# Raw weight pairs of the gated layer: two alternating pairs of buffers in place of one, and an earlier place for their loads

## The chip, the cores and the metric

The kernel runs on one core of a Trainium2 chip. The metric is the device time of one execution in microseconds (us). The kernel before takes 925.53 us (median of three runs, 925.38 to 925.86).

## What is computed

Three stages follow one another: retention (attention with a decay in place of the softmax), a feed-forward layer with the Mish function, and a gated feed-forward layer (SwiGLU). All is float32.

```python
scores = q @ k.T / sqrt(64)                       # 4 batches, 8 heads, 576 positions
ret = scores * Dmat                               # causal, gamma[h] ** (i - j)
x = (ret @ v), heads joined                       # [2304, 512]
h = x @ w_in                                      # [512, 2048]
x = (h * tanh(softplus(h))) @ w_out               # [2048, 512]
g = x @ w_gate;  val = x @ w_val                  # [512, 1536] each
out = (silu(g) * val) @ w_out2                    # [1536, 512]
```

## The kernel before

**Numbers in two parts.** TensorE multiplies a rounded float32 format. So every factor is split into a high and a low part, and a product is three matmuls. ScalarE makes the high part (a cast), VectorE the low one (a subtraction).

**Four stretches of time.** First comes retention. Then come the slots `slot(s)` of the first layer, up to s = 63: each does one first-layer product (12 matmuls, L610) and one older second product (12 matmuls, L644), some 4.2 us together. Then come the *joint blocks* `pair1(i)`, i = 0 to 7 (L914). They compute the last two token blocks of the first layer together, by a Strassen scheme of seven products in place of eight. Product c of pair i is six matmuls at L839 into a PSUM tile `te`; after it a few waiting matmuls of the second product (L881, mostly 9 or 12) are taken from a list. The last stretch is the gated layer, also by Strassen (L1057, tiles `t`).

**What hangs on a product of a joint block.** Three PSUM tiles rotate through two buffers. Each product c is followed by one operation that empties or reads its tile: a ScalarE copy (c = 0), a Mish on ScalarE (c = 2) or an addition on VectorE (L846, c = 1, 3, 4, 5, 6). The product two places later (c + 2) can't begin before that operation is done.

**Weights of the gated layer.** Each Strassen product needs a combination of weight blocks, in two parts. These are made ahead of time on ScalarE and VectorE, in pieces strewn between the first layer's work, and stored to device memory (`comb`); the gated layer reads them back. `group(n)`, n = 0 to 11, prepares one pair of raw weight tiles, gate (even n) or value (odd n). Its `load` issues two 512 KB loads (L186) into the buffers `raw0` and `raw1`. Its steps are: two `rebias` steps (L114 on ScalarE, L115 on VectorE, on the raw words), two times `sign` and `join` (L119, L123), and then puts and combinations in turn. A put (L189) casts into one of four `c` tiles on ScalarE (L191), subtracts on VectorE (L192), and has SyncE write the tile to `comb` (L193). A group puts seven: a11 and a12, a22, s1 and s3, s2 and s4.

**Who else has raw buffers.** There are four, `raw0` to `raw3`. `last(n)`, n = 0 to 3, prepares one weight tile of the last product in `raw2`. `group1(i)`, i = 0 to 7, makes combinations of the first layer's weights and uses `raw3` as scratch (`e`).

**Order and pace.** The order on every queue is written out by hand: what the program emits first runs first on its engine. `pieces()` (L276) strings the groups together. Each step has a price; `Pace` (L292) gets a credit per slot or per product (2.0 per slot, 1.2 per slot from s = 51 on and per product of pairs 1 to 7) and emits steps while the credit lasts. A step of price 0.0 (the loads) is emitted as soon as it is reached. A group's twelve steps cost 8.6; the load of the next group follows them, and then `gap`, two empty steps of 0.8, before the next group's first `rebias`. By these prices group 6 ends in slot 60, group 7 runs from slot 62 to product (1,5), that is pair 1, c = 5, and groups 8 to 11 fill products (2,0) to (6,4). `group1(7)` ends in slot 58.

**The SyncE queue** issues all of these transfers in one order: the raw loads, the writes to `comb`, and the loads of the first layer's stored combinations (`eu`, L720, 512 KB, one after every second product, six tiles ahead). An instruction that waits there holds up all behind it.

Of the kernel before, what the change touches and what calls it, by code (L numbers as in the profile page):

```python
# [16 lines left out]
def retention_mish_swiglu(  # L17
# [48 lines left out]
    def cols(w, i):  # L66
        return w.bitcast(U32)[:, i * 256:(i + 1) * 256].rearrange("(k p) f -> p k f", p=128)
# [18 lines left out]
    def place(kind, i, shape, dtype, name):  # L86
        j = home[kind, i]
        return pools["a" if j < NA else "b"].tile(shape, dtype, tag=f"u{j}", name=name)

    def words(j):  # L90
        w = raw[j].rearrange("p (n t) -> p n t", t=2)
        return w[:, :, 0], w[:, :, 1]
# [19 lines left out]
    def rebias_raw(j):  # L112
        lo, hi = words(j)
        nc.scalar.activation(hi.bitcast(F32), hi.bitcast(F32), AF.Copy, scale=2.0 ** -112)  # L114
        nc.vector.tensor_scalar(lo, lo, 29, None, op0=ALU.logical_shift_right)  # L115

    def sign(j):
        lo, hi = words(j)
        nc.vector.scalar_tensor_tensor(lo, hi, 0x80000000, lo, op0=ALU.bitwise_and, op1=ALU.bitwise_or)  # L119

    def join(j):
        lo, hi = words(j)
        nc.vector.scalar_tensor_tensor(lo, hi, 3, lo, op0=ALU.logical_shift_left, op1=ALU.bitwise_or)  # L123
# [60 lines left out]
    def raw_load(key, src, whole, n):  # L184
        raw[key] = rp.tile([128, 2 * DM], U32, tag=f"raw{n}", name=f"raw{key}")
        nc.sync.dma_start(out=raw[key] if whole else raw[key].rearrange("p (k f) -> p k f", k=KT), in_=src)  # L186


    def put(x, dst, nm, eng):  # L189
        c = pools["c"].tile([128, 2, KH], F32R, tag="c", name=nm)  # L190
        nc.scalar.copy(out=c[:, 0, :], in_=x)  # L191
        eng.tensor_tensor(out=c[:, 1, :], in0=x, in1=c[:, 0, :].bitcast(F32), op=ALU.subtract)  # L192
        nc.sync.dma_start(out=dst, in_=c.bitcast(F32))  # L193
# [5 lines left out]
    def combine(v, names):  # L199
        for o, a, b, op in ADDS:  # L200
            if o in names:
                nc.vector.tensor_tensor(out=v[o], in0=v[a], in1=v[b], op=op)

    def group(n):
        i, z = divmod(n, 2)
        keys = [f"{'gv'[z]}{i}_{e}" for e in range(2)]
        v = {}

        def load():
            for e in range(2):  # L210
                raw_load(keys[e], cols((w2_gate, w2_val)[z], 2 * i + e), False, e)
                lo, hi = words(keys[e])
                for h in range(2):
                    v[f"a{e + 1}{h + 1}"] = lo[:, h * KH:(h + 1) * KH].bitcast(F32)
                    v["s" + "1324"[2 * e + h]] = hi[:, h * KH:(h + 1) * KH].bitcast(F32)

        def puts(*names):
            for nm in names:
                c = z * NG + USES.index(nm)
                put(v[nm], comb[i][c // 2][:, c % 2], f"c{i}_{c}", nc.vector)  # L220

        return load, [
            (0.55, lambda: rebias_raw(keys[0])), (0.55, lambda: rebias_raw(keys[1])),
            (0.7, lambda: sign(keys[0])), (0.7, lambda: join(keys[0])),
            (0.7, lambda: sign(keys[1])), (0.7, lambda: join(keys[1])),
            (0.85, lambda: puts("a11", "a12")), (0.85, lambda: combine(v, ("s1", "s3"))),
            (0.45, lambda: puts("a22")), (0.85, lambda: combine(v, ("s2", "s4"))),
            (0.85, lambda: puts("s1", "s3")), (0.85, lambda: puts("s2", "s4")),
        ]
# [29 lines left out]
            (0.85, lambda: combine(v, ("s2", "s4"))), (0.85, lambda: puts("s2", "s4")),  # L259
        ]  # L260

    FIRST = 4

    def last(i):
        key = f"f{i}"

        def puts():
            x = words(key)[0].bitcast(F32)
            for h in range(DM // KH):
                put(x[:, h * KH:(h + 1) * KH], find[i][:, :, h * KH:(h + 1) * KH], f"f{i}_{h}", nc.gpsimd)  # L270

        return lambda: raw_load(key, rows(w2_out, i), True, 2), [
            (0.6, lambda: rebias_raw(key)), (0.7, lambda: sign(key)), (0.7, lambda: join(key)), (0.2, puts),
        ]

    def pieces():  # L276
        gr = [group(n) for n in range(2 * PAIRS)]
        gap = [(0.8, lambda: None)] * 2
        for n, (load, steps_) in enumerate(gr):
            f_load, behind = last(n) if n < FIRST else (None, gap)  # L280
            if n == 0:
                yield 0.0, load
                yield from gap
            yield from steps_[:2]
            if f_load:
                yield 0.0, f_load
            yield from steps_[2:]
            if n + 1 < len(gr):
                yield 0.0, gr[n + 1][0]
            yield from behind  # L290

    class Pace:  # L292
# [3 lines left out]
        def __call__(self, more):  # L296
            self.left += more
            while self.ahead and self.left >= self.ahead[0]:
                self.left -= self.ahead[0]
                self.ahead[1]()  # L300
                self.ahead = next(self.todo, None)

    second = Pace(pieces())
    third = Pace(x for i in range(F1 // 2) for x in group1(i))

# [297 lines left out]
    with tc.manual_schedule():  # L603
# [128 lines left out]
        def fin_load(i):  # L732
            at_ = ("in", 1 + i) if i < 8 else ("out", 4 + i)
            fu[i] = place(*at_, [128, 2, DM], F32R, f"fu{i}")
            if i < FIRST:
                nc.sync.dma_start(out=fu[i].bitcast(F32), in_=find[i])

        def fin_raw(i):
            if i < F2:
                key, shape = f"f{i}", [128, 2 * DM]  # L740
                raw[key] = place("in", 9, shape, U32, f"raw{key}") if i % 2 else pools["rx"].tile(
                    shape, U32, tag="rx", name=f"raw{key}"
                )
                nc.sync.dma_start(out=raw[key], in_=rows(w2_out, i))

        def fin_step(u, c):
            n = FIRST + 2 * (u - 1)
            i, k = divmod(c, 4) if c < 4 else (1, c - 3)
            i += n
            key = f"f{i}"  # L750
            if k == 0:
                rebias_raw(key)
            elif k == 1:
                sign(key)
            elif k == 2:
                join(key)
                fin_load(i)
                nc.scalar.copy(out=fu[i][:, 0, :], in_=words(key)[0].bitcast(F32))
            else:
                nc.vector.tensor_tensor(  # L760
                    out=fu[i][:, 1, :], in0=words(key)[0].bitcast(F32), in1=fu[i][:, 0, :].bitcast(F32), op=ALU.subtract
                )
                fin_raw(i + 2)
            if c == 3:
                rebias_raw(f"f{n + 1}")
# [236 lines left out]
        later += rests  # L1002
        for i in range(FIRST):
            fin_load(i)
        fin_raw(FIRST)
        fin_raw(FIRST + 1)
        nc.scalar.preload_act_table_set("silu_and_others")
# [109 lines left out]
        for u in range(NS2):  # L1117
            i = u % PAIRS
            if i == PAIRS - 2 and u + 2 < NS2:
                n = u // PAIRS + 1  # L1120
# [65 lines left out]
```

## Time and profile before

| | us |
|---|---|
| median of three runs | 925.53 |
| the profiled execution | 924.93 |
| its span, first to last instruction | 923.1 |
| TensorE busy | 906.4 (98%) |
| VectorE busy | 564.0 (61%) |
| ScalarE busy | 379.5 (41%) |
| span of the joint blocks, first `te` product to first `t` product | 357.2 to 490.3 |

The profile is of one execution. The page gives each engine's busy time; a weight load (PEld) runs beside the matmuls (PE), so both are near full where TensorE is never idle. The timeline lists instructions in order of time; in square brackets stands how long the engine was idle before one, and what released it. The windows give the engines' busy time in chosen stretches. An operation's duration includes its latency, and operations in a row overlap by some 0.1 us.

### The profile page before, as it was taken

The numbers are of one execution on the slowest core, as the hardware profiler recorded it, in microseconds if no ns is written. First come the engines' busy times: TensorE is split into PE (matmuls) and PEld (weight loads), VectorE is DVE, ScalarE is ACT, GpSimd is POOL, SyncE is SP. The second block draws the span as 40 slices with busy tenths as digits, with TensorE's granted clock in tenths as the row PEclk, the third lists the DMA queues.
The fourth block names the chain that finished last, engine by engine and source line by source line (L and its number), as shares of the span: only waits on it lengthen the run. The fifth ranks groups of instructions, "written<-read, shape, count | busy, mean of one in ns | idle before, by whom it ended". The sixth has DMA issues, their size and how long they took to land.

```text
span 923.1 us, 15226 instructions
## 1 busy us (share of the span) xinstructions
PE 906.4 (98%) x5828; PEld 862.3 (93%) x5828; DVE 564.0 (61%) x1094; ACT 379.5 (41%) x790; POOL 58.3 (6%) x55
## 2 busy tenths in 40 slices
PE   8999999999999999998999999999999999999998
PEld 8888999999999999988999999999999999999997
DVE  3878599468867773555684666656544556544444
ACT  3767466355555544434454333324222223222222
POOL 3654200000000000000000000000000000000000
PEclk9999999999999999999999999999999999999999
DMA  9999265267876636577657566544644444654421
GB/s 213 252 256 235 70 185 181 80 205 264 281 253 229 234 140 219 194 252 264 227 194 296 175 211 202 187 155 159 218 160 158 163 156 164 219 160 160 160 92 68
DMA packets 125016, 177.58 MB, mean 192 GB/s; under 512 B 46352, under 2 KB 83984, under 8 KB 124944
## 3 DMA queue, kind: packets, MB, share of 16 engines
q1 hardware_dynamic: 123840, 176.19, 61.0%
q8 instruction: 46, 0.75, 0.3%
q10 hardware_dynamic: 1104, 0.42, 0.2%
q14 instruction: 26, 0.21, 0.1%
HBM read 133.07 MB, written 43.52 MB: 191 GB/s over the span
## 4 chain that ended last, share of the span: by engine, by line
PE 82%; DMA 6%; DVE 6%; ACT 3%; issue 1%; SPq 1%; DVEq 0%; ACTq 0%
PE t L839 28%; PE fa L1019 16%; PE h L610 14%; PE acc L644 13%; PE te L839 3%; PE ea L881 3%; PE o L513 2%; DMA rawg<-in_moe_w_gate_dram 1%; DMA rawv<-in_moe_w_val_dram 1%; DMA q<-in_q_dram 1%; DMA raw<-in_moe_w_out_dram 1%; PE acc L852 1%; PE s L437 1%; DMA comb<-c 1%; PE o L504 1%
## 5 line engine op out<-in xcount | busy, mean ns | idle before, releaser
L839 PE MATMUL t<-y,su 128*128 128x384 f32 x1512 | 306.7, 338 | 1.1 <-ACT p L1091 0.6
L839 PEld LDWEIGHTS t<-y,su 128*128 128x128 f32 x1512 | 270.8, 188 | 24.4 <-DVE cv L846 1.8
L1019 PE MATMUL fa<-fu,g 128*128 128x512 f32 x648 | 190.2, 395 | 0.1
L610 PE MATMUL h<-xs,u 128*128 128x384 f32 x768 | 143.7, 336 | 0.0
L644 PE MATMUL acc<-g,u 128*128 128x384 f32 x720 | 134.6, 336 | 0.4 <-DVE u L134 0.4
L610 PEld LDWEIGHTS h<-xs,u 128*128 128x128 f32 x768 | 133.9, 188 | 0.4
L644 PEld LDWEIGHTS acc<-g,u 128*128 128x128 f32 x720 | 125.8, 188 | 0.7 <-DVE u L134 0.7
L1019 PEld LDWEIGHTS fa<-fu,g 128*128 128x128 f32 x648 | 118.5, 188 | 7.7 <-ACT g L1042 0.5
L1042 ACT CAST g<-sg 128x384 fp32r<-128x384 f32 x72 | 37.0, 513 | 173.2 <-DVE sg L1078 120.5
L881 PE MATMUL ea<-ge,u 128*128 128x256 f32 x576 | 77.3, 281 | 0.0
L881 PEld LDWEIGHTS ea<-ge,u 128*128 128x128 f32 x576 | 75.4, 189 | 0.0
L839 PE MATMUL te<-ye,eu 128*128 128x384 f32 x336 | 68.4, 338 | 6.0 <-DVE ve L846 2.8
L672 DVE TENSOR_TENSOR g<-m,g 128x384 fp32r<-128x384 f32 x64 | 36.0, 563 | 60.1 <-ACT g L668 60.0
L1067 ACT ACTIVATE sg<-sg 128x384 f32<-128x384 f32 x54 | 28.4, 526 | 90.9 <-DVE sg L846 90.9
L1047 DVE TENSOR_TENSOR g<-sg,g 128x384 fp32r<-128x384 f32 x72 | 40.2, 558 | 40.7 <-ACT g L1042 40.7
L839 PEld LDWEIGHTS te<-ye,eu 128*128 128x128 f32 x336 | 56.9, 188 | 7.0 <-DVE ve L846 3.2
L661 ACT ACTIVATE m<-h 128x384 f32<-128x384 f32 x64 | 31.2, 488 | 66.7 <-PE h L610 66.7
L846 DVE TENSOR_TENSOR u<-t,p 128x384 f32<-128x384 f32 x36 | 20.0, 556 | 44.2 <-PE t L839 41.4
L846 DVE TENSOR_TENSOR v<-t,p 128x384 f32<-128x384 f32 x36 | 20.0, 556 | 35.4 <-PE t L839 34.7
L668 ACT CAST g<-m 128x384 fp32r<-128x384 f32 x64 | 32.9, 513 | 1.8
L1078 DVE TENSOR_TENSOR sg<-sg,cv 128x384 f32<-128x384 f32 x54 | 30.2, 558 | 1.9
L123 DVE SCALAR_TENSOR_TENSOR raw<-raw 128x512 uint32<-128x512 uint32 x32 | 27.2, 851 | 0.0
(117 smaller groups left out, 968.2 us busy)
## 6 DMA issues: line engine op xcount, KB each, us to landing
su<-comb SPq DMA_DIRECT2D x126, 512.0 KB, 3.3
comb<-c SPq DMA_DIRECT2D x84, 256.0 KB, 2.5
eu<-ecomb SPq DMA_DIRECT2D x28, 512.0 KB, 4.8
raw<-in_moe_w_in_dram SPq DMA_DIRECT2D x16, 512.0 KB, 5.3
raw<-in_moe_w_out_dram SPq DMA_DIRECT2D x16, 512.0 KB, 4.1
ecomb<-e_s SPq DMA_DIRECT2D x32, 256.0 KB, 2.3
rawg<-in_moe_w_gate_dram SPq DMA_DIRECT2D x12, 512.0 KB, 5.2
ecomb<-u SPq DMA_DIRECT2D x24, 256.0 KB, 3.2
```

What stands on the lines that cost most here:

```text
L610: nc.tensor.matmul(ps, lhsT=u[:, a, kk * 128:(kk + 1) * 128], rhs=s[:, e, :], start=(c == 0), stop=(c == n - 1),)
L644: nc.tensor.matmul(accs[b][d][:, :T], lhsT=u[:, a, d * 128:(d + 1) * 128], rhs=g[:, e, :], start=(i == 0 and c == 0), stop=(i == F1 - 1 an ...
L661: nc.scalar.activation(w, hs.pop(s), AF.Mish)
L668: nc.scalar.copy(out=gs[s][:, 0, :], in_=ws[s])
L672: nc.vector.tensor_tensor(out=g[:, 1, :], in0=ws.pop(s), in1=g[:, 0, :].bitcast(F32), op=ALU.subtract)
L839: nc.tensor.matmul(p, lhsT=w[:, a, kk * 128:(kk + 1) * 128], rhs=y[kk][:, x, :], start=begin and kk == 0 and (a, x) == (0, 0), stop=kk == ...
L846: nc.vector.tensor_tensor(out=out_, in0=a, in1=b_, op=ALU.add)
L881: nc.tensor.matmul(o, lhsT=u[:, a, d * 128:(d + 1) * 128], rhs=y, start=f == 0 and (a, x) == (0, 0) and (r == 0 or r == 2 and d % 2 == 0), ...
L1019: nc.tensor.matmul(accs["f", b][m], lhsT=gs[u, e, h][:, x, m * 128:(m + 1) * 128], rhs=fu[2 * (u % PAIRS) + e][:, a, :], start=first, stop ...
L1042: nc.scalar.copy(out=gs[u, e, h][:, 0, :], in_=x)
L1047: nc.vector.tensor_tensor(out=g[:, 1, :], in0=x, in1=g[:, 0, :].bitcast(F32), op=ALU.subtract)
L1078: later.append(lambda: nc.vector.tensor_tensor(out=y, in0=y, in1=x, op=ALU.mult))
```

## The change

Up to group 6 nothing is different. The raw pairs of groups 7, 9 and 11 go to `raw2` and `raw3`, those of 8 and 10 stay with `raw0` and `raw1`. The load of group n + 1 is emitted at the beginning of group n (n from 7 on) and no longer behind its last put, and the two empty steps between the groups 7 to 11 are gone. The load of group 7 stays where it was.

```diff
@@ -208,7 +208,7 @@
         def load():
             for e in range(2):
-                raw_load(keys[e], cols((w2_gate, w2_val)[z], 2 * i + e), False, e)
+                raw_load(keys[e], cols((w2_gate, w2_val)[z], 2 * i + e), False, e + 2 * (n >= FREE and n % 2))
                 lo, hi = words(keys[e])
@@ -259,7 +259,7 @@
-    FIRST = 4
+    FIRST, FREE = 4, 7
@@ -281,11 +281,14 @@
             if n == 0:
                 yield 0.0, load
                 yield from gap
+            if n >= FREE and n + 1 < len(gr):
+                yield 0.0, gr[n + 1][0]
+                behind = []
             yield from steps_[:2]
             if f_load:
                 yield 0.0, f_load
             yield from steps_[2:]
-            if n + 1 < len(gr):
+            if n < FREE:
                 yield 0.0, gr[n + 1][0]
             yield from behind
```

## Rows read from the trace of the kernel before

**Rows 1.** The page: busy time of TensorE, and its granted clock in 40 slices

```profile
PE 906.4 (98%) x5828; PEld 862.3 (93%) x5828; DVE 564.0 (61%) x1094; ACT 379.5 (41%) x790; POOL 58.3 (6%) x55
PEclk9999999999999999999999999999999999999999
```

**Rows 2.** Windows: stretch, length, busy us per engine (instructions), clock, DMA share, GB/s

```profile
375.00:490.00 115.00, 108.99 (x776) 107.98 (x775) 72.75 (x161) 51.08 (x114) 0.00 (x0) 1.00 0.68 224
465.00:480.00 15.00, 15.00 (x109) 15.00 (x108) 12.54 (x28) 7.32 (x17) 0.00 (x0) 1.00 0.68 225
490.00:510.00 20.00, 19.43 (x139) 19.23 (x138) 8.40 (x18) 8.66 (x19) 0.00 (x0) 1.00 0.85 321
510.00:910.00 400.00, 399.36 (x2067) 369.79 (x2066) 212.23 (x396) 108.49 (x219) 0.00 (x0) 1.00 0.51 167
```

**Rows 3.** Timeline of weight loads in the joint blocks: the five with idle time

```profile
396.26 1.00 PEld L839 LDWEIGHTS te<-ye,eu 128*128 128x128 f32 x6 [1.55 <-DVE scratch L846]
415.81 1.00 PEld L839 LDWEIGHTS te<-ye,eu 128*128 128x128 f32 x6 [1.16 <-ACT we L923]
438.56 1.00 PEld L839 LDWEIGHTS te<-ye,eu 128*128 128x128 f32 x6 [2.58 <-DVE ve L846]
452.98 0.99 PEld L839 LDWEIGHTS te<-ye,eu 128*128 128x128 f32 x6 [0.58 <-DVE ve L846]
458.42 1.00 PEld L839 LDWEIGHTS te<-ye,eu 128*128 128x128 f32 x6 [1.15 <-DVE scratch L846]
```

**Rows 4.** Timeline around the third of them, all engines

```profile
430.04 1.68 SPq L186 DMA_DIRECT2D rawg<-in_moe_w_gate_dram  x2
...
432.84 1.23 PE L881 MATMUL ea<-ge,u 128*128 128x256 f32 x9
...
433.91 1.21 PE L839 MATMUL te<-ye,eu 128*128 128x384 f32 x6
...
434.95 1.23 PE L881 MATMUL ea<-ge,u 128*128 128x256 f32 x9
...
436.12 0.43 DVE L115 TENSOR_SCALAR rawg<-rawg 128x512 uint32<-128x512 uint32 x1 [4.52 <-DMA rawg<-in_moe_w_gate_dram]
...
437.61 0.43 DVE L115 TENSOR_SCALAR rawg<-rawg 128x512 uint32<-128x512 uint32 x1 [1.06 <-DMA rawg<-in_moe_w_gate_dram]
437.95 0.55 DVE L846 TENSOR_TENSOR ve<-te,ve 128x384 f32<-128x384 f32 x1
...
438.56 1.31 PE L839 MATMUL te<-ye,eu 128*128 128x384 f32 x6 [2.38 <-DVE ve L846]
...
439.71 1.23 PE L881 MATMUL ea<-ge,u 128*128 128x256 f32 x9
```

**Rows 5.** Waits of VectorE from 355 to 490: total us, times, longest

```profile
DVE rawg L115 <- DMA rawg<-in_moe_w_gate_dram: 10.2, 4, 4.5
DVE rawv L115 <- DMA rawv<-in_moe_w_val_dram: 10.2, 3, 5.5
```

**Rows 6.** Raw gate loads from 385 to 460: issue to landing

```profile
DMA to landing us min/median/max: 5.0/6.0/6.9
```

**Rows 7.** Raw value loads from 385 to 475: issue to landing

```profile
DMA to landing us min/median/max: 4.6/5.7/6.7
```

**Rows 8.** Last reader of `raw3` as scratch: durations (ns), first and last start

```profile
L192 DVE TENSOR_TENSOR e_s<-e,e_s x32: 413/419/428, 190.1 to 336.3; 128x256 fp32r<-128x256 f32 x32
```

**Rows 9.** SyncE's timeline: the raw load of group 7

```profile
346.64 1.35 SPq L186 DMA_DIRECT2D rawv<-in_moe_w_val_dram  x2
```

**Rows 10.** ScalarE's timeline: the two puts that waited for a `c` tile

```profile
428.40 0.44 ACT L191 CAST c<-rawv 128x256 fp32r<-128x256 f32 x1 [1.45 <-DMA comb<-c]
...
451.58 0.42 ACT L191 CAST c<-rawg 128x256 fp32r<-128x256 f32 x1 [2.95 <-DMA comb<-c]
```

**Rows 11.** The chain of waits: start, length, the write that the second one waited for

```profile
446.28 5.23 DMA comb<-c
```

**Rows 12.** All 35 writes of `c` tiles from 370 to 475: issue to landing

```profile
DMA to landing us min/median/max: 2.0/2.7/5.5
```

## Prediction

> **What bounds the kernel now.** I read the page first. TensorE is busy for 906.4 of 923.1 us, and its granted clock is full in every slice [rows 1], so what can be won is the time in which it stands idle, and nothing is to be had from its clock. Next I read the windows, to see where that idle time lies. In the gated layer TensorE works 399.36 of 400 us, from 490 to 510 it works 19.43 of 20, but in the stretch of the joint blocks that the change touches only 108.99 of 115 [rows 2]. So 6.0 us of idle time lie there, and all that follows runs at TensorE's pace: a microsecond that a joint block ends earlier is a microsecond at the end.
>
> The timeline of the weight loads then shows this idle time as five single gaps, 1.55, 1.16, 2.58, 0.58 and 1.15 us long, with next to nothing between them [rows 3]. Each ends on VectorE or ScalarE, on the operation that frees a PSUM tile. That is the name in brackets, not yet the cause. The cause is one step further back, and the third gap shows it [rows 4]: the raw load of group 10 is issued at 430.04, VectorE reaches the first rebias on it and stands 4.52 us until 436.12, another 1.06 us for the second tile of the pair, and only then, at 437.95, does the addition `ve` run, whose product had ended at 435.1 at the latest (433.91 + 1.21). TensorE takes up the product that waited for it at 438.56. Engines run their queues in order, so a rebias whose data is late holds the addition behind it, and the addition holds TensorE. The waits list gives the sum for VectorE: seven waits on raw loads, 20.4 us [rows 5]. The first, second and fifth gap come right after such a wait too (groups 8, 9 and 11). The fourth, 0.58 us, is another thing: a put that waited 2.95 us for a free `c` tile [rows 10].
>
> Why is the data late? The load is issued behind the last put of the group before, because it needs that group's buffers, and the two empty steps cost 1.6 credits, 1.33 products at 1.2 a product. A product with its 9 matmuls of L881 takes 2.11 us (from 432.84 to 434.95 [rows 4]), so the first rebias comes about 2.8 us after the issue. The loads land after 5.0 to 6.9 and 4.6 to 6.7 us [rows 6, 7]. What is missing, 2 to 4 us, exceeds the one product of slack that an addition has.
>
> **What the change removes.** For groups 8 to 11 the load is asked for one whole group earlier. A group's steps cost 8.6 credits, 7.2 products, 15 us at 2.11 us a product. The longest landing is 6.9 us, so no rebias of these groups should wait, with 8 us to spare. Gone are then gaps one, two, three and five: 1.55 + 1.16 + 2.58 + 1.15 = 6.44 us by the weight loads. Measured from start to start the third gap is a little more: from the L881 matmuls at 434.95 to the product at 438.56 pass 3.61 us, where the undisturbed pair 432.84 and 433.91 has 1.07, which makes 2.54; and the delayed product takes 1.15 us until the next L881 instead of 1.04, which makes 2.65 in all. That is 0.07 above its weight-load gap; four times this gives 6.7 us. I take 6.7.
>
> **What it moves, and what stands behind that.** Load 8 moves from product (1,5) to slot 62, loads 9 to 11 from the end to the beginning of groups 8 to 10. On SyncE each of these two issues moves past a group's seven writes to `comb` and the `eu` loads between them. It adds a wait there only if the buffer is not free. Loads 9, 10 and 11 need the buffers of the group just finished; the write of that group's last put stands directly in front of them on SyncE and waits for the same VectorE subtraction, so nothing is added. Load 7 goes to `raw2` and `raw3`: `raw3` was last read at 336.3 [rows 8], ten microseconds before load 7 is issued at 346.64 [rows 9], and `raw2` long before. If it did block, the `eu` loads behind it would be held; with six tiles of lead that cover lasts twelve products. Cost: nothing.
>
> **What it adds: density.** Without the empty steps groups 8 to 11 end at product (5,6) and no longer (6,4): the same instructions in five products less, about 11 us. Bound from above: all 72.75 us of VectorE's work in the 115 us stretch [rows 2], in a stretch shorter by 6.7 and 11 us, is 75% busy. The trace shows 84% (12.54 of 15 us) with TensorE busy for 15.00 [rows 2]. So the density as such should be bearable. Its bounds are a gain of nothing (there is no idle time left to win) and a loss of one gap of the fourth kind in each of the four groups, 4 x 0.6 us.
>
> The fourth kind needs care. There are four `c` tiles and seven puts, so the put of s4 takes the tile of a22, two products earlier, and waits until that write has landed. Of these writes one took 5.23 us [rows 11] against a median of 2.7 [rows 12]; it was issued behind an `eu` load in the same product. By the prices a22 now falls on products (2,3), (3,3), (4,3), (5,3); the `eu` loads come with odd 7i + c, so (2,3) and (4,3) have one in front. Before, groups 9 and 10 had. In one of these the wait was 1.45 us and cost TensorE nothing, in the other, where all four last puts fall in one product, 2.95 us and 0.58 us of TensorE [rows 3, 10]. The new schedule again has one of either kind: group 8 with its puts in two products, group 10 with all four in product (4,5). So I keep the 0.6 us and add 0.3 for (4,5), where TensorE's products are of the short kind (2.11 us) and give less slack.
>
> The Trainium skill ("DMA: Bandwidth & Descriptors", section "Queues, rings and completion order") says that each DMA engine consumes the descriptors of one issuing queue in ring order; by that a write to `comb` that stands behind two freshly issued raw loads would have to wait for them, and an early load would make the puts worse. By the schedule this doesn't bite: the first put of a group comes five products, over 10 us, behind the raw load in front of it, and the longest landing is 6.9 us [rows 6].
>
> **Sum.** 6.7 gained, 0.3 lost: 6.4 us. The profiled execution's 924.93 us (span 923.1 and 1.8 us around it) would become 918.5; the median of the runs lies 0.6 higher, so 925.5 - 6.4 = 919.1.
>
> **Rivals.**
> - *Half of it comes back.* The puts and the sign and join steps now follow without a pause, and the waits for `c` tiles cost 0.6 to 0.9 us in each of groups 8 to 11, 2.4 to 3.6 us instead of 0.6: 921.5 to 922.5. For it: the empty steps were the only places where VectorE could catch up. Against it: the 84% stretch without a gap.
> - *No change.* VectorE would be late by its own load wherever it was late by the DMA, and each gap is replaced by another of the same size: 925.5. It needs VectorE nearly full over these 70 us; 75% speaks against it. That the change doesn't do what it says (a load blocked behind a buffer, and the rebias waits as before) ends here too; the ten microseconds of `raw3` and the order on SyncE speak against it.
> - *Slower.* The place is the put of s4. With loads and writes closer together in the one SyncE queue, every a22 write lands as late as the one of [rows 11] or later, and ScalarE, holding the put, holds the Mish and casts behind it and VectorE's subtraction. Beyond the 2.95 us of [rows 10] every further microsecond goes to TensorE in full. To eat the 6.7 us and 1.9 more in four groups, 0.6 of which is there already, each must cost 2.3 us, so wait 4.7 us, so the write must take 6.9 us to land. That is the point where it decides; the longest of 35 took 5.5 [rows 12]. It would give 927.5 and more.
>
> **How the numbers follow.** Forecast 0.71, half back 0.16, no change 0.09, slower 0.04. A measurement of this kernel can tell about 0.2%, 1.9 us, from no change, so the first two are faster (0.87), the third the same, the last slower. The range reaches at the low end to the case that the fourth gap goes as well and the run-to-run 0.2 us is added (925.5 - 7.3 - 0.3 = 917.9), and at the high end to the half-back case, 922.5; it leaves out the last two cases.
>
> **What would show it.** Right: no waits of L114 or L115 on raw loads between 385 and 480, the last conversions some 18 us earlier than before (5 products, and the gaps gone), TensorE busy to within 1 us of that stretch, gaps of L839 only behind a put that waits for `comb<-c`, and the stretches from the first gated product on as long as before. Wrong: rebias waits that remain (the loads are not early), or new gaps in front of L839 that end on L846 while VectorE was busy throughout (density), or behind L191 in every group (tiles). An `eu` load that ends a gap would mean that the moved loads took the bandwidth.

## The result, and the profile after

| | before | after |
|---|---|---|
| median, four runs each | 925.69 us (925.38 to 926.21) | 916.72 us (916.26 to 917.38) |
| ratio, with 95% interval | | 0.9903 (0.9886 to 0.9920) |
| profiled execution, and its span | 924.93, 923.1 | 916.83, 915.0 |
| joint blocks, first `te` to first `t` product | 133.1 us (357.2 to 490.3) | 125.8 us (356.5 to 482.3) |
| gated layer, first to last `t` product | 422.0 us | 421.9 us |

The changed kernel is faster, by 9.0 us in these medians; the forecast was 6.4, 919.1, with a range from 917.9 to 922.5. The direction and the place were right; the size was not, and the time lies 1.2 us below the range.

The first two lines are the page's busy times and granted clock, as in [rows 1]; the others are windows as in [rows 2] (stretch, length, busy us of PE, PEld, DVE, ACT, POOL with their instructions, clock, DMA share, GB/s).

```profile
PE 904.5 (99%) x5828; PEld 861.5 (94%) x5828; DVE 565.7 (62%) x1094; ACT 378.2 (41%) x790; POOL 57.0 (6%) x55
PEclk9999999999999999999999999999999999999999
```
```profile
357.00:482.00 125.00, 125.00 (x875) 125.00 (x875) 82.17 (x178) 58.52 (x132) 0.00 (x0) 1.00 0.65 221
490.00:510.00 20.00, 19.86 (x127) 19.14 (x126) 9.49 (x19) 4.86 (x13) 0.00 (x0) 1.00 0.69 253
510.00:902.00 392.00, 391.50 (x2026) 362.61 (x2025) 207.13 (x387) 107.32 (x217) 0.00 (x0) 1.00 0.51 167
```

In the joint blocks TensorE is now busy for 125.00 of 125 us, where [rows 2] had 108.99 of 115. All five gaps of [rows 3] are gone, the fourth among them. The timeline of the weight loads has no line with idle time from 350 until the first products of the gated layer:

```profile
487.64 1.01 PEld L842 LDWEIGHTS t<-y,su 128*128 128x128 f32 x6 [0.77 <-ACT p L1094]
504.66 0.30 PEld L1022 LDWEIGHTS fa<-fu,g 128*128 128x128 f32 x2 [0.46 <-ACT g L1045]
```

SyncE's timeline shows the moved loads. Load 8 (`rawg`, 348.55) follows load 7 with only two `eu` loads between them, and load 9 (387.90) is issued one group ahead of its use at 402.67, the first of the two `rebias` lines of ScalarE that follow. The third line is VectorE's `rebias` of group 10, the one before which VectorE stood 4.52 us in the kernel before [rows 4]. None of the three has idle time before it:

```profile
345.94 1.34 SPq L186 DMA_DIRECT2D rawv<-in_moe_w_val_dram  x2
347.38 1.12 SPq L723 DMA_DIRECT2D eu<-ecomb  x2
348.55 1.47 SPq L186 DMA_DIRECT2D rawg<-in_moe_w_gate_dram  x2
...
387.90 1.07 SPq L186 DMA_DIRECT2D rawv<-in_moe_w_val_dram  x2
```
```profile
402.67 0.69 ACT L114 ACTIVATE rawv<-rawv 128x512 f32<-128x512 f32 x1
405.05 0.67 ACT L114 ACTIVATE rawv<-rawv 128x512 f32<-128x512 f32 x1
...
419.94 0.76 DVE L115 TENSOR_SCALAR rawg<-rawg 128x512 uint32<-128x512 uint32 x2
```

VectorE's last subtraction for a put (L192) begins at 452.22, where it began at 471.49: 19.3 us earlier, where some 18 were forecast.

The transfers themselves did not get faster: in after the gate loads issued from 380 on, and then the value loads, land in these times (compare [rows 6, 7]).

```profile
DMA to landing us min/median/max: 6.1/6.6/7.0
```
```profile
DMA to landing us min/median/max: 5.1/5.8/6.3
```

So the joint blocks gained 7.3 us between the two profiled executions, 0.7 us lies before them (the first joint product begins at 356.5 and no longer at 357.2), and only 0.1 us lies behind them. Two questions were open: why 7.3 and not 6.4, and where the 0.9 us come from by which the medians differ by more than the profiled executions (9.0 against 8.1).

### The profile page after: what moved, and what is told of

It is laid out like the page before. It is cut to its first block, busy times and chain, and to the rows that moved or that the text cites. A ratio compares the mean times of both kernels' runs of the same rounds, so it can differ in the third digit from the quotient of the medians.

```text
span 915.0 us, 15212 instructions
## 1 busy us (share of the span) xinstructions
PE 904.5 (99%) x5828; PEld 861.5 (94%) x5828; DVE 565.7 (62%) x1094; ACT 378.2 (41%) x790; POOL 57.0 (6%) x55
## 4 chain that ended last, share of the span: by engine, by line
PE 90%; DVE 4%; DMA 2%; ACT 2%; issue 1%; SPq 0%; ACTq 0%; DVEq 0%
PE t L842 28%; PE fa L1022 16%; PE h L613 14%; PE acc L647 13%; PE ea L884 7%; PE te L842 6%; PE o L516 2%; DMA q<-in_q_dram 1%; DMA raw<-in_moe_w_out_dram 1%; PE s L440 1%; PE acc L855 1%; PE o L507 1%; DVE p L449 1%; DVE raw L123 1%; PE tk L424 0%
## 5 line engine op out<-in xcount | busy, mean ns | idle before, releaser
L647 PEld LDWEIGHTS acc<-g,u 128*128 128x128 f32 x720 | 125.8, 188 | 0.7 <-DVE u L134 0.7
```

Of the source, the lines that this page charges most:

```text
L647: nc.tensor.matmul(accs[b][d][:, :T], lhsT=u[:, a, d * 128:(d + 1) * 128], rhs=g[:, e, :], start=(i == 0 and c == 0), stop=(i == F1 - 1 an ...
```

## The experiments

The joint blocks' time is the measure in all of them, since the change acts there; it is taken from the first start of a `te` product to that of a `t` product, in the profiled execution of each kernel.

| kernel | median us | joint blocks us | mean granted clock, profiled execution |
|---|---|---|---|
| before | 925.69 | 133.1 | 0.999 |
| after | 916.72 | 125.8 | 1.000 |
| rep_before | 925.52 | 135.8 | 0.996 |
| rep_after | 917.25 | 125.8 | 1.000 |
| early_gap | 916.98 | 125.9 | 0.999 |
| late_nogap | 948.11 | 154.6 | 0.987 |
| long_gap | 919.94 | 126.8 | 1.000 |
| lead3 | 917.56 | 125.8 | 0.999 |
| two_pairs_late (one execution) | 924.24 | 133.3 | 0.999 |
| stall_vector | 919.95 | 128.4 | 1.000 |
| stall_v8 | 927.77 | 136.4 | 1.000 |
| stall_v12 | 943.79 | 153.6 | 0.987 |
| after_c3 (one execution) | 935.83 | 127.9 | 0.991 |
| after_table | 916.84 | 125.8 | 0.998 |

### Both kernels again

> The kernel before, once more. The prediction counted 6.7 us of gaps in one profiled execution; the change gained 9.0 in the medians (925.69 to 916.72) and 8.1 between the two profiled executions. Theory 1 (chance outside the joint blocks): here the joint blocks take the same 133 us again, and the rest of the difference is in the first 157 us, where first products start some tenths of a us apart. Theory 2 (the gaps vary): the joint blocks take 133 to 135 us, as the landings of the raw loads differ from execution to execution, and the median stands for longer gaps than the profile that was read. Time: ratio 1.000 to the kernel before by both.

> The changed kernel, once more: 916 to 917.5 us. Theory 2 says that the joint blocks take 125.8 us again to within 0.2, since no wait on a transfer is left in them; theory 1 says the same, but that the time from the start to the first joint product (356.5 us in the profile of after, 357.2 in that of before) differs between this and the copy of before only by chance.

Measured: 925.52 (921.77 to 927.2) against 925.28 for the runs beside it, ratio 0.9996 (0.9983 to 1.0009); after 917.25 (916.76 to 918.2), ratio 0.9906 (0.9891 to 0.9922). The joint blocks of the copy of after take 125.8 us again, those of the copy of before 135.8, 2.7 us more than in the profile that I had read. Neither theory had the reason. The gaps are about as long, four of them, 6.66 us in all:

```profile
396.33 1.31 PEld L839 LDWEIGHTS te<-ye,eu 128*128 128x128 f32 x6 [1.94 <-DVE scratch L846]
417.27 0.99 PEld L839 LDWEIGHTS te<-ye,eu 128*128 128x128 f32 x6 [1.02 <-ACT we L923]
439.77 1.00 PEld L839 LDWEIGHTS te<-ye,eu 128*128 128x128 f32 x6 [2.34 <-DVE ve L846]
460.75 1.00 PEld L839 LDWEIGHTS te<-ye,eu 128*128 128x128 f32 x6 [1.36 <-DVE scratch L846]
```

The fourth gap, behind the put, is absent here. But six weight loads take 1.31 us behind the first gap where they take 1.00 elsewhere. The windows of this copy tell why (the last three numbers are the granted clock, the DMA share and GB/s):

```profile
390.00:396.30 6.30, 4.59 (x34) 4.39 (x33) 1.35 (x4) 1.68 (x3) 0.00 (x0) 1.00 0.95 317
396.30:400.30 4.00, 3.97 (x18) 3.97 (x19) 3.93 (x8) 1.34 (x4) 0.00 (x0) 0.58 0.33 105
400.30:437.40 37.10, 36.29 (x260) 36.08 (x259) 19.76 (x46) 14.12 (x33) 0.00 (x0) 1.00 0.74 243
437.40:441.50 4.10, 1.97 (x14) 1.76 (x13) 3.01 (x7) 2.33 (x4) 0.00 (x0) 0.97 0.77 293
441.50:446.00 4.50, 4.50 (x23) 4.50 (x23) 3.47 (x9) 3.19 (x8) 0.00 (x0) 0.64 0.01 4
```

Behind the first gap TensorE's granted clock is 0.58 for 4 us, that is mostly the lower of its two levels (1.2 GHz), and 18 matmuls run in 4 us where the same stretch of the first profile of before has 28 at clock 1.00. Behind the third gap it is 0.64 for 4.5 us. Those two stretches cost 4.0 x 0.42 + 4.5 x 0.36 = 3.3 us of full-speed work, and 125.8 + 6.7 + 3.3 = 135.8 is the time measured. So a third theory was formed: a gap costs its own length, and in part of the executions TensorE's clock falls behind it as well. In this execution it did; how much that is worth in the medians is taken up further down. The forty slices of the page hide it: all of them read 9 in this execution too.

### Which half of the change does it

```diff
# early_gap (from after): the empty steps put back
-                behind = []
# late_nogap (from before): the empty steps taken out of groups 7 to 11
-            yield from behind
+            if n < 7 or n + 1 == len(gr):
+                yield from behind
# two_pairs_late (from before): the alternating buffers alone
-                raw_load(keys[e], cols(...), False, e)
+                raw_load(keys[e], cols(...), False, e + 2 * (n >= 7 and n % 2))
```

> The changed kernel with the two empty steps (1.6 credits) between groups 7 to 11 put back: the loads alone are early. If the lead of the load is all: no rebias waits, joint blocks 125.8 us, time as after (916.7, ratio 0.990). If the empty steps cost something by themselves (the conversions end five products later, beside the first preparations of the gated layer): 0.5 to 1 us slower than after. If the fourth gap (put of s4 waiting for a c tile) belongs to the schedule with empty steps and not to the raw wait before it, 0.6 us of it remains, joint blocks 126.4.

> The kernel before with the two empty steps between groups 7 to 11 taken out, one pair of buffers, load behind the last put: the other part of the change alone. If the lead of the load is all: each rebias comes 1.33 products, 2.8 us, earlier behind its load, so each of the four gaps grows by up to 2.8 us: joint blocks about 144 us, time about 936 us (ratio 1.012). If the empty steps were themselves what TensorE lost: 920 or less.

> The kernel before with the alternating buffers alone: the raw pairs of groups 7, 9 and 11 in raw2 and raw3, each load behind the last put of the group in front and both empty steps kept. If the lead of the load is all: joint blocks 132 to 136 us, 922 to 928 us, as the kernel before in its executions. If it was the sharing of one pair that held the load on SyncE (waiting for its readers): the load issues earlier, gaps shorter, 920 or less.

Measured. With early loads (and the second pair of buffers that they need) and the empty steps kept, 916.98 us and joint blocks of 125.9: the early load gives all of the gain, taking out the empty steps is worth nothing. The fourth gap is absent here too, though the puts stand in the same products as in the kernel before; one put waits 1.2 us for a `c` tile and no gap follows. With the empty steps taken out and late loads, 948.11 us: right in sign, but 12 us above the 936 expected. The gaps grew by 1.5 to 4.9 us each (up to 2.8 was expected), to 20.2 us in all, and of the 28.8 us by which the joint blocks are longer than those of after, 8.6 are not idle time. The clock is the rest: six weight loads take 1.78 us behind three of the four gaps, and in the windows behind the first and the third gap the granted clock is 0.50 and 0.74.

```profile
394.65 1.78 PEld L840 LDWEIGHTS te<-ye,eu 128*128 128x128 f32 x6 [4.94 <-DVE scratch L847]
418.98 1.78 PEld L840 LDWEIGHTS te<-ye,eu 128*128 128x128 f32 x6 [6.09 <-DVE scratch L847]
443.52 1.26 PEld L840 LDWEIGHTS te<-ye,eu 128*128 128x128 f32 x6 [4.04 <-ACT scratch L948]
466.13 1.78 PEld L840 LDWEIGHTS te<-ye,eu 128*128 128x128 f32 x6 [5.12 <-ACT scratch L948]
```
```profile
394.70:399.50 4.80, 4.80 (x19) 4.80 (x20) 4.13 (x8) 1.92 (x4) 0.00 (x0) 0.50 0.41 138
443.50:450.00 6.50, 6.47 (x35) 6.47 (x36) 4.83 (x10) 1.99 (x5) 0.00 (x0) 0.74 0.28 103
```

The alternating buffers alone change nothing: 924.24 us in one execution, joint blocks of 133.3, the same five gaps (1.47, 1.23, 2.42, 0.49, 1.46).

### How much lead is enough

```diff
# long_gap (from before): longer pauses, one pair of buffers
             yield from behind
+            if 6 < n < len(gr) - 1:
+                yield 2.0, lambda: None
# lead3 (from after): the load three steps ahead of the group's end
-                yield 0.0, gr[n + 1][0]
                 behind = []
...
-            yield from steps_[2:]
+            yield from steps_[2:9]
+            if n >= FREE and n + 1 < len(gr):
+                yield 0.0, gr[n + 1][0]
+            yield from steps_[9:]
```

> The changed kernel with each load of groups 8 to 11 moved back behind the ninth step of the group in front, so that 2.55 credits, 2.1 products, 4.5 us lie between the issue and the first rebias. Landings take 5 to 7 us, so rebias waits of 0.5 to 2.5 us; by the slack of one product (2.1 us) TensorE loses nothing or a few tenths at a time: joint blocks 125.8 to 127 us, time 917 to 918.5. If every wait on a raw load costs TensorE, 4 x 1.5 = 6 us: 923.

> The kernel before with 2.0 more credits of empty steps between groups 7 to 11: one pair of buffers, loads late in the queue as before, but 3 products (6.3 us) and no longer 1.33 (2.8 us) between the issue of a raw pair and its first rebias. If the lead of the load is all: rebias waits of at most 1 us, below the one product of slack, no gap in front of L839 in the joint blocks, joint blocks 125.8 to 126.5 us, time 916.7 to 917.5 us without any second pair of buffers. If the second pair or the missing pauses matter by themselves: slower than after by over 1 us.

Measured: the joint blocks of lead3 take 125.8 us, as with leads of 15 us and more in after. The lead was not 4.5 us, though. That figure comes from the prices; in time 5.8 to 6.4 us pass between the issue of a load and VectorE's first `rebias` on it, here for group 9:

```profile
398.14 1.17 SPq L186 DMA_DIRECT2D rawv<-in_moe_w_val_dram  x2
...
403.98 0.42 DVE L115 TENSOR_SCALAR rawv<-rawv 128x512 uint32<-128x512 uint32 x1
...
406.30 0.43 DVE L115 TENSOR_SCALAR rawv<-rawv 128x512 uint32<-128x512 uint32 x1 [0.97 <-DMA rawv<-in_moe_w_val_dram]
```

The landings took 4.3 to 7.7 us. Rebias waits remain (1.0 us on VectorE, 0.7 on ScalarE in all), and TensorE loses nothing; the run as a whole is 917.56 us because its first joint product begins at 357.3. With longer pauses and a single pair of buffers the gaps in front of `te` vanish as well: VectorE comes to the first `rebias` 3.1 us behind the issue in group 8 and waits 2.0 us, ScalarE waits up to 3.6, and no gap follows. But the time is 919.94. The joint part of the expectation held, the time missed by 3 us, and the timeline shows where: the conversions end later (VectorE's last subtraction for a put begins at 483.16, right in front of the addition that ends the first of these gaps), beside the preparations of the gated layer.

```profile
484.44 1.00 PEld L841 LDWEIGHTS t<-y,su 128*128 128x128 f32 x6 [1.00 <-DVE scratch L848]
487.48 1.01 PEld L841 LDWEIGHTS t<-y,su 128*128 128x128 f32 x6 [0.85 <-DVE scratch L848]
491.21 1.00 PEld L841 LDWEIGHTS t<-y,su 128*128 128x128 f32 x6 [1.18 <-ACT p L1093]
```

Two new gaps and a longer third; joint blocks and gated layer together take 2.4 us more than in after (126.8 + 423.4 against 125.8 + 422.0), the other 1 us lies before the joint blocks (first `te` product at 357.6). So the second pair of buffers is not what removes the waits, but it buys the lead without a pause.

### A gap without any transfer

To test the clock apart from the raw loads, VectorE was held up with work in the changed kernel: the step that computes s1 and s3 is done several times over in groups 8 to 11.

```diff
-            (0.85, lambda: combine(v, ("s1", "s3"))),
+            (0.85, lambda: [combine(v, ("s1", "s3")) for _ in range(R if n > 7 else 1)]),
# stall_vector: R = 5, stall_v8: R = 8, stall_v12: R = 12
```

> The changed kernel with VectorE held up by work in place of a transfer: in groups 8 to 11 the step that computes s1 and s3 is done five times in place of once, eight additional VectorE operations of 0.4 us, 3.2 us in a row, in four places; the result is the same. TensorE should get four gaps of 1.2 to 2 us, 5 to 8 us in all, as long as those of the kernel before, with no wait on a raw load. If what the medians gained beyond the gaps (1.7 us) was TensorE's clock falling to 1.2 GHz after a gap in part of the executions: here too the granted clock is below full behind some gaps, the mean clock of the runs lies at 0.997 to 0.999 and the joint blocks are longer than 125.8 plus the gaps by 1 to 3 us; 923 to 927 us, with a spread of 2 us or more. If it was varying landings alone: clock 1.000, the gaps the same in every execution, spread below 1 us.

> The changed kernel with VectorE held up longer: the step for s1 and s3 done eight times in groups 8 to 11, 14 additional operations of 0.34 us, 4.7 us in a row. Three more repetitions than the run before add 2.0 us to each hold, so the gaps of TensorE grow from 0.2 to 0.6 us to 2 to 2.6 us, as long as the longest of the kernel before. If TensorE's clock falls behind gaps of that length whatever caused them: mean clock 0.995 to 0.999, different from run to run, granted clock below full for some us behind one or more of the gaps, joint blocks 125.8 + 9 + 1 to 4 us, time 926 to 930. If the clock of the kernel before fell for another reason (the transfers): clock 1.000, joint blocks 135, time 926 with a spread below 1 us.

> The same with twelve repetitions, 22 additional operations, 7.4 us in a row: gaps of 4.5 to 5.5 us, as long as those of the kernel without empty steps and with late loads, whose mean clock was 0.987. If the gap alone lowers the clock: mean clock 0.985 to 0.989 in every run, each gap followed by some us at 1.2 GHz, joint blocks 125.8 + 20 + 8 = 154 us, time 944 to 948. If the transfers had to do with it: clock 0.999 or more, joint blocks 146 us, time 937.

Measured. R = 5: eight operations took 2.7 us, not 3.2, and the slack swallowed most; gaps of 0.22 to 0.59 us, 2.0 in all, joint blocks 128.4, 919.95 us, clock full. These gaps are too short to decide anything about the clock; the expected 5 to 8 us of gaps were a miss. R = 8: a gap of 1.8 to 2.3 us behind each of the four holds and some short ones, 9.8 us in all, joint blocks 136.4. Its five runs, by their mean clock:

```
clock 1.000: 927.19, 927.20, 927.77     clock 0.999: 928.14     clock 0.998: 929.12
```

The order fits the clock, and a fall of 0.002 over 925 us, 1.9 us, is what the slowest has over the fastest. But in the profiled one the clock stayed full, and where it fell in the other two can't be seen: after_table, which has no gap in its joint blocks, has a mean clock of 0.998 as well, by a fall in its retention (0.99 from 30 to 160 us). So R = 8 leaves the case open. R = 12: gaps of 4.5 to 5.0 us, 18.6 in all, but the joint blocks grow by 27.8. The windows of each gap and what follows it:

```profile
398.70:403.70 5.00, 0.25 (x3) 0.05 (x1) 5.00 (x16) 0.00 (x0) 0.00 (x0) 0.91 0.07 27
403.70:408.50 4.80, 4.79 (x18) 4.79 (x19) 3.69 (x9) 2.51 (x6) 0.00 (x0) 0.50 0.35 123
408.50:424.00 15.50, 15.50 (x109) 15.50 (x108) 11.60 (x28) 5.45 (x13) 0.00 (x0) 0.96 0.75 250
424.00:429.00 5.00, 0.67 (x7) 0.46 (x5) 5.00 (x16) 0.04 (x1) 0.00 (x0) 0.77 0.00 0
429.00:434.00 5.00, 5.00 (x20) 5.00 (x21) 3.29 (x9) 3.37 (x8) 0.00 (x0) 0.54 0.78 261
```

TensorE stands idle while VectorE is full (5.00 of 5 us) and the transfers rest (shares of 0.07 and 0.00), and then runs for 5 us at 0.50 and 0.54. So the clock falls behind a gap of this length without any transfer. By rows alone: behind the gaps of 4.0 to 6.1 us of late_nogap and stall_v12 it fell each time in the profiled executions (and the mean clock is 0.986 to 0.990 in all eight executions of the two). Behind gaps of 1.8 to 2.6 us in the joint blocks it fell in one profiled execution (the copy of before) and not in four others (before, two_pairs_late, stall_v8, after_c3), and no fall is seen there behind the gaps of up to 1.6 us. For gaps of about 2 us, whether transfers play a part is not decided.

The Trainium skill ("TensorE: Matmul & The Clock Gate", section "HAM oscillation — how this bites in real kernels") describes a matmul loop whose waits for transfers let the clock drop, so that the penalty is paid again at each wait. The runs here agree (0.50 to 0.74 in the windows behind such gaps of rep_before and late_nogap), and they show that a wait on VectorE does the same.

### The fourth gap, and a version that might beat both

```diff
# after_c3
-tile_pool(name="pc", bufs=4
+tile_pool(name="pc", bufs=3
# after_table: preload_act_table_set("silu_and_others") moved from behind the handover
#              of the pools to right behind the last pair1(i)
```

> The changed kernel with three c tiles in place of four: the put of s4 now waits for the write of s1, one product or less in front of it. Landings of 2.0 to 4.6 us leave waits of 1 to 3 us in ScalarE in each of groups 8 to 11. By the slack that the runs have shown so far (3.2 us of VectorE held cost 0.2 to 0.6 us of TensorE) the joint blocks become 126 to 128 us, time 917 to 919.5. If a put that waits costs TensorE as the prediction priced it (all beyond 2.4 us of wait, 0.6 at 2.95): the same range, at its upper end.

> The changed kernel with the load of ScalarE's function table for the gated layer (1.28 us) emitted right behind the last Mish of the joint blocks, ahead of four casts. In the changed kernel TensorE idles 0.57 us behind the first ScalarE copy of a gated product, which stands behind that table load. Expected: that gap gone, 916.1 us, 0.6 us faster than after, which five rounds can just tell. Rival: the table load holds the casts, which TensorE needs next, and the gap moves: no difference or 0.5 us slower.

Measured: with three `c` tiles the whole time is 935.83, because the slots ahead of the joint blocks use the same tiles: the first joint product begins at 373.3 and no longer at 356.5. I had not thought of them. From 190 to 373 ScalarE waits 14.6 us for `c` tiles and TensorE's weight loads stand idle for 12.1 us; the longest gap is 7.68 us, and the clock falls to 0.50 behind it. It falls there as well behind a gap of 1.70 us that comes close behind one of 0.63; TensorE does 1.00 us of work in the 2.76 us of the two gaps and then runs at 0.60:

```profile
227.00:229.76 2.76, 1.00 (x5) 0.43 (x3) 1.35 (x4) 1.65 (x5) 0.00 (x0) 1.00 0.61 168
229.76:232.00 2.24, 2.24 (x8) 2.24 (x9) 2.17 (x5) 0.00 (x0) 0.00 (x0) 0.60 1.08 371
```

Inside the joint blocks, the part that was to be tested, five puts wait 6.2 us in all, up to 2.83. The longest of these waits is followed by TensorE's one gap, of 1.81 us, and the blocks take 127.9 us: at the upper end of what was expected. A put that waits does cost TensorE, but only sometimes, and then more than the prediction's price (all beyond 2.4 us of wait) would give for it, 0.4 us.

```profile
453.96 0.42 ACT L191 CAST c<-rawg 128x256 fp32r<-128x256 f32 x1 [2.83 <-DMA comb<-c]
...
455.35 1.00 PEld L842 LDWEIGHTS te<-ye,eu 128*128 128x128 f32 x6 [1.81 <-DVE scratch L849]
```

The moved table load gives nothing: 916.84 us, the gap of 0.78 us at 487.83 remains. The casts that I wanted behind the load had been emitted before that place already, as ScalarE's timeline shows: the load (L996) is still behind them and ahead of the copy that TensorE waits for.

```profile
485.06 0.93 ACT L795 CAST y<-y 128x384 fp32r<-128x384 f32 x2
486.01 1.28 ACT L996 ACT_TABLE_LOAD   x1
487.30 0.48 ACT L1094 COPY p<-t 128x384 f32<-128x384 f32 x1
```

No kernel here beats after beyond the uncertainty.

## Why the prediction was right in kind and wrong in size

**The bound and the place: right.** TensorE bounds the kernel, and the joint blocks' gain comes through to the end undiminished: 7.3 us there, 0.7 in front, the gated layer 421.9 against 422.0.

**The four gaps of the raw loads: right.** They are gone, by the lead of the load: early_gap has all of the gain, two_pairs_late none, long_gap loses the gaps with one pair of buffers, and lead3 shows that leads of 5.8 to 6.4 us suffice for landings of 4.3 to 7.7 us. Four gaps at 6.7 us and the fourth-kind gap at 0.6 make 7.3, the gain of the joint blocks in the profiled pair; so the term itself was sized well for that execution. The explanation of why the data was late was not exact: the "about 2.8 us" from the issue to the first rebias came from the prices. In the trace VectorE stood at that rebias 0.4 to 1.6 us behind the issue and waited 3.5 to 5.5 us. The sum did not use the 2.8.

**The fourth gap: the wrong step (0.9 us).** "So I keep the 0.6 us and add 0.3" took the puts to be as far apart as the prices say, two products. They are that in the program, not in time. These are the lines of the kernel before: ScalarE's cast of a22, SyncE's write, and three of the four last casts.

```profile
444.59 0.43 ACT L191 CAST c<-rawg 128x256 fp32r<-128x256 f32 x1
...
446.28 0.32 SPq L193 DMA_DIRECT2D comb<-c  x1
...
447.57 1.07 ACT L191 CAST c<-rawg 128x256 fp32r<-128x256 f32 x3
```

Only 2.4 us behind the write, at 448.6, ScalarE is at the put that needs the tile back, and the write lands after 5.23 us [rows 11]. VectorE and ScalarE were catching up on what the raw load of group 10 had held, and the steps followed one another without the time between. With early loads and the same places in the program (early_gap) the lines are these, with all four last casts:

```profile
436.62 0.42 ACT L191 CAST c<-rawg 128x256 fp32r<-128x256 f32 x1
...
438.31 0.32 SPq L193 DMA_DIRECT2D comb<-c  x1
...
441.54 1.40 ACT L191 CAST c<-rawg 128x256 fp32r<-128x256 f32 x4
```

The last of the four starts about 442.5, 4.2 us behind the write, which here took 4.1 us to land, and waits for nothing. Of the 2.95 us that the put waited before, 1.8 went by the greater distance and the rest by the faster landing. So in the profile of before the fourth gap was a consequence of the raw wait 15 us before it, together with a late landing. The raw wait alone doesn't bring it: in the copy of before (rep_before) the put came 3.9 us behind a write that landed after 4.2, waited 0.36 us, and no gap followed. The 0.3 us for product (4,5) did not come either: no put of after costs TensorE anything. That the density is bearable was judged rightly, and its two rivals (half back, slower) did not come true.

**The clock: a step that was missing, of a size that stays open.** "Nothing is to be had from its clock" was read off the forty slices of one execution, in which the clock happened to stay full behind gaps of up to 2.58 us. In the copy of before it did not, and there the falls cost an estimated 3.3 us. For the average the records decide less. In 46 executions of the kernel before (its own repeats and the runs beside the experiments) the mean granted clock is 0.9983; in 20 executions of the kernels without a gap in the joint blocks (after, rep_after, early_gap, lead3, after_table) it is 0.9994. If all of that difference lay where TensorE sets the pace, it would be 1.0 us of 920. The times don't bear this out. The six executions of before at 1.000 have a mean of 924.95, still 7.9 us above the mean of 917.1 of the ten gap-free ones at 1.000, and the 25 of before at 0.998 have one of 925.2, only 0.2 more where a loss of 0.002 would be 1.9. And after_table, which lost its clock in the retention, took 916.99 us at 0.998. So these means give the clock a few tenths of the gain rather than 1.0 us; since the executions of one clock value spread by 1.5 to 5 us, its share stays open.

**The rest of the 9.0 us.** The mean times of before (46) and after (8) are 925.2 and 917.1 us, 8.1 apart, like the profiled pair. Some 0.9 of the 9.0 is thus the luck of four executions on either side: before's median lies 0.5 above the larger mean, after's 0.35 below. Of the 8.1, the joint blocks are 7.3 in the profiled pair. The other 0.8, 0.7 of it in front of the joint blocks, was not separated: the first joint product begins between 356.1 and 357.6 in all of the profiled kernels but after_c3, with early loads and without.

**The range.** Its low end allowed for all five gaps and for 0.3 us of noise, 917.9; the three runs known then lay within 0.5 us. That noise was sized too small: executions of before lie between 921.8 and 927.8, with a standard deviation of 1.2 us, those of after between 916.3 and 918.2. With the fourth gap in the sum the forecast would have been 918.2 (925.5 - 7.3); the mean of after's eight executions is 1.1 us lower, of which the records explain only part. The high end has a slip in it: the sum already kept the 0.6 us and the 0.3, so 2.4 to 3.6 us in place of 0.6 would have given 920.6 to 921.8, not 921.5 to 922.5.

## What to carry to other kernels

When an engine works through its queue in order, look up, for every instruction that waits on a transfer, what stands behind it: here the late load cost nothing by itself, the addition behind it held the matmuls, and even a put 15 us later was delayed by the catching up. What is needed is lead between the issue of a load and the first use, about its landing time (waits of up to 2.0 us that were left cost TensorE nothing here), and a second buffer buys it more cheaply than a pause. Measure such distances in the trace: in a hand-written order, steps that are two products apart by their prices were one apart in time. A gap in front of TensorE can cost more than its length: look at the granted clock right behind each gap, in windows of a few microseconds and in several executions, before you write that the clock is full.

## What the runs showed of the hardware

- TensorE's granted clock fell to its lower level for some 3 to 6 us behind idle gaps of 4.0 to 6.1 us, each time in the two profiled executions that have them (stall_v12, late_nogap). Behind gaps of about 2 us it fell in some executions and not in others: it fell in rep_before behind 1.94 and 2.34 us and in after_c3 behind 1.70 us (close behind 0.63), and it stayed full in the first profile of before behind 2.58 us.
- With such a fall a gap of 5 us cost some 7 us (27.8 us for the four of stall_v12, of which 18.6 are idle).
- The page's slices of 23 us hide such a fall: the clock line of rep_before reads 9 throughout, at a mean clock of 0.996.
- A hold of 2.7 us on VectorE cost TensorE 0.2 to 0.6 us at a time (stall_vector), one of 4.7 us some 2 us (stall_v8): about one product of slack, which takes 2.1 to 2.5 us.
- Raw loads of 512 KB took 4.3 to 7.7 us from issue to landing in before, after and lead3.
